# Second mixture of experts in hand order: raw weight pages loaded over a whole expert, split half an expert later

## The chip, the cores and the metric

The kernel runs on one core of one Trainium2 chip. The metric is the device time of one execution in microseconds; of several runs the median is given. A run's profile gives the span from the first to the last instruction and the granted clock of TensorE, as a share of its full 2.4 GHz.

## The reference

Windowed attention (window 64, 4 x 8 heads of 576 rows, head size 64) gives `x` of 2304 tokens by 512. A first, dense gated layer (`silu(xn @ w_gate) * (xn @ w_val) @ w_out` after an RMS norm) follows, and then the part that is changed, a second layer of eight experts of which each token takes two:

```python
logits = x @ w_gate
noise_scale = np.log1p(np.exp(x @ w_noise))
noisy_logits = logits + noise_scale * noise
top2 = np.argpartition(-noisy_logits, 2, axis=1)[:, :2]
...
for e in range(E):
    for k in range(2):
        mask = top2[:, k] == e
        ...
        h = np.maximum(x[mask] @ w1[e], 0.0)
        out[mask] += top2_w[mask, k, None] * (h @ w2[e])
```

Here `w1[e]` is 512 x 1024 and `w2[e]` 1024 x 512, in float32.

## The kernel before

Each float32 product is made of three matmuls in a faster format: an operand is split into a high part H (ScalarE copies it into that format) and a low part L (VectorE subtracts), and H*H, H*L and L*H are added up in PSUM. So every weight page that arrives raw (`st`, 128 x 1024) has to be split by ScalarE (`wH`, line 593) and then VectorE (`wL`, line 594) before TensorE can use it. The pages come from one pool of 24 (`page`); an expert has four raw pages of `w1` (i = 0 to 3) and four of `w2` (i = 4 to 7), which become 16 split pages. A page is free again when its last reader is done.

After the router, experts are taken by falling count, each with a fixed number of token slots: 640, 704, 640, 560, 560, 544, 544, 544. Position 0 is always expert 0. For position `e` there are these steps:

- `load_tb`: GpSimd fetches the table of token numbers and weights of the expert (`tb`); VectorE turns the numbers into integers (`tid`).
- `gather(e, t)`: GpSimd fetches 128 token rows (`xg`, L632); `xg_t(e, t)`: TensorE transposes them (`xgt`, L660), ScalarE writes their H part (`xph`, L663) and VectorE the L part (`xpl`, L664). For expert 0 these are `xah`/`xal` (first 384 slots) and `xbh`/`xbl` (the rest).
- `mm1(e, fc, blk)`: first product, L686, twelve matmuls into one PSUM bank `h` for 128 of the 1024 hidden columns and one half of the tokens; 16 such groups per expert. ScalarE (L693) and VectorE (L694) evict it as `hh`. Five banks are shared by these groups and by `xgt`.
- `mm2(e, t)`: second product of one tile of 128 tokens, L855, 24 matmuls of 512 columns into `y`; ScalarE scales it into `ys` (L862); GpSimd scatters it by a DMA that adds to `out` (L863). The scatters of different tiles add to the same tensor, so each waits for the one before.

An expert has five tiles (six at position 1), the last one with 32 to 64 tokens. The raw pages of experts 1 to 7 are loaded by GpSimd's indirect DMA (L584), those of expert 0 by SyncE.

Engines execute their own queues in order. What stands in the queues is set by a scheduler with a timeline model that reorders the program; the code below gives it only data dependencies and a program order to start from. In that order an expert's `mm2` tiles alternate with load and split of the next expert's `w1`, and `w2` follows behind the last tile:

```python
        for t in range(tiles(e + 1) if nx else len(left)):
            if left:
                mm2(e, left.pop(0))
            if nx:
                if t < 4:
                    load_split(e + 1, t)
                xg_t(e + 1, t)
```

Of the kernel before, what the change touches and what calls it, by code (L numbers as in the profile page):

```python
# [23 lines left out]
def tile_window_attention_swiglu_top2(  # L24
# [45 lines left out]
    def page(dt, name):  # L70
        return pages.tile([P, 1024], dt, name=name, tag="pg", bufs=NPG)
# [6 lines left out]

# [1 line left out]
    ident = consts.tile([P, P], F32, name="ident")  # L80
# [42 lines left out]

# [1 line left out]
    RG = 3 * WIN  # L125
# [16 lines left out]
    RT = (13, 14, 16, 17, 20)  # L142
    M2 = (2, 2)
    FL = (0, 0, 0, 1, 0, 0, 2)
# [128 lines left out]

# [1 line left out]
    xnH, xnL = {}, {}  # L275
# [52 lines left out]

# [1 line left out]
    gv, wo = {}, {}  # L330
# [101 lines left out]

# [1 line left out]
    XS, XTT, LZ = {}, {}, {}  # L434
# [136 lines left out]

# [1 line left out]
    W1, W2 = {}, {}  # L573
# [3 lines left out]

    def load_split(e, i):
        st = page(F32, f"st{e}_{i}")
        src, c = (w1r, i) if i < KD else (w2r, i - KD)  # L580
        if e == 0:
            nc.sync.dma_start(st, src[c * P:(c + 1) * P, :])
        else:
            nc.gpsimd.indirect_dma_start(out=st, out_offset=None, in_=src,  # L584
                                         in_offset=bass.IndirectOffsetOnAxis(ap=wi[:, e, c:c + 1], axis=0))
        h, l = page(F32R, f"wH{e}_{i}"), page(F32R, f"wL{e}_{i}")
        if i < KD:
            a, ho, lo = (x.rearrange(r, **{k: 2, "m": P}) for x, r, k in
                         ((st, "p (c m k) -> p c k m", "k"), (h, "p (c k m) -> p c k m", "k"),
                          (l, "p (c k m) -> p c k m", "k")))  # L590
        else:
            a, ho, lo = st, h, l
        nc.scalar.activation(ho, a, AF.Copy)  # L593
        nc.vector.tensor_tensor(lo, a, ho.bitcast(F32), op=ALU.subtract)  # L594
        if i < KD:
            W1[e, i] = (h, l)
        else:
            for k in range(2):
                W2[e, 2 * (i - KD) + k] = (h[:, 512 * k:512 * k + 512], l[:, 512 * k:512 * k + 512])

    XG, XH = {}, {}
# [15 lines left out]
    def load_tb(e):  # L617
# [3 lines left out]
        else:  # L621
            nc.gpsimd.indirect_dma_start(out=t.rearrange("p c w -> p (c w)"), out_offset=None,
                                         in_=table.rearrange("(p c) w -> p (c w)", c=NT1),
                                         in_offset=bass.IndirectOffsetOnAxis(ap=tbi[:, e:e + 1], axis=0))
        i = w2p.tile([P, 8], I32, name=f"tid{e}", tag="tid", bufs=2)
        nc.vector.tensor_copy(i[:, :tiles(e)], t[:, :tiles(e), 0])
        TB_[e], TID[e] = t, i

# [67 lines left out]

# [1 line left out]
    load_qk(0)  # L698
# [146 lines left out]
    def mm2(e, t):  # L845
# [5 lines left out]
        for fc in range(NF2):  # L851
            hh = HH[e, fc, part]
            h, l = W2[e, fc]
            for a, b in ((hh[:, 0, c], h), (hh[:, 0, c], l), (hh[:, 1, c], h)):
                nc.tensor.matmul(ps[:m], a, b, start=i == 0, stop=i == 3 * NF2 - 1)  # L855
                i += 1
        if e == 0 and t < TA:
            y, w, r = page(F32, f"ysa{t}")[:, :DM], ta[:, t, 1:2], tia[:, t:t + 1]
        else:
            y = w2p.tile([P, DM], F32, name=f"ys{e}_{t}", tag="ys", bufs=3)  # L860
            w, r = TB_[e][:, t, 1:2], TID[e][:, t:t + 1]
        nc.scalar.activation(y[:m], ps[:m], AF.Copy, scale=w[:m])  # L862
        nc.gpsimd.indirect_dma_start(  # L863
            out=out, out_offset=bass.IndirectOffsetOnAxis(ap=r[:m], axis=0),
# [6 lines left out]
    for fc in first:  # L871
        mm1(0, fc, 0)
    for t in range(M2[0]):
        mm2(0, t)
    main.close()

# [1 line left out]
    w2p = ctx.enter_context(tc.tile_pool(name="moe2", bufs=1, reuse_waits="tile"))  # L878
    V = nc.vector
    load_tb(0)  # L880

# [1 line left out]
    def row(name, n=E, dt=F32):  # L883
# [35 lines left out]

# [1 line left out]
    def count_beyond():  # L921
# [75 lines left out]


    for t in range(TA, tiles(0)):
        gather(0, t)  # L1000
    for t in range(M2[0], M2[1]):
        mm2(0, t)
    for t in range(TA, tiles(0)):
        xg_t(0, t)
    for t in range(M2[1], TA):
        mm2(0, t)
    for fc in range(NF2):
        mm1(0, fc, 1)
    for e in range(E):
        nx = e + 1 < E  # L1010
        if e > 0:
            for fc in range(NF2):
                for blk in range(2):
                    mm1(e, fc, blk)
        for kk in range(KD):
            W1.pop((e, kk))
        if nx:
            load_tb(e + 1)
            for t in range(tiles(e + 1)):
                gather(e + 1, t)  # L1020
        else:
            count_beyond()
        left = list(range(TA if e == 0 else 0, tiles(e)))
        for t in range(tiles(e + 1) if nx else len(left)):
            if left:
                mm2(e, left.pop(0))
            if nx:
                if t < 4:
                    load_split(e + 1, t)
                xg_t(e + 1, t)  # L1030
        for t in left:
            mm2(e, t)
        if nx:
            for i in range(4, 8):
                load_split(e + 1, i)

# [33 lines left out]
```

## Time and profile before

| | before |
|---|---|
| runs, us | 1153.52, 1159.80, 1159.81 |
| median, us | 1159.8 |
| span of the profiled execution, us | 1152.4 (no other time of that execution is recorded) |
| mean granted TensorE clock | 0.974 |
| TensorE busy | 1071.3 us, 93% of the span |
| VectorE, ScalarE, GpSimd busy | 53%, 48%, 38% |
| first product of expert 1 begins | 706.5 us into the span |

The page's slices show TensorE at nine tenths nearly throughout; what lies between two slices has to be looked for in the views of waits and in the timeline. In a timeline row the first number is the start, the second the length (of several merged instructions together), and the bracket tells how long the engine had been idle before it and what released it. "xN" is a number of merged instructions. Matmuls overlap, so the pace of TensorE is the distance from one start to the next, not the length.

### The profile page before, as it was taken

To read this page: it belongs to the slowest core of one execution; us is meant where nothing else is said; L and a number is where in the kernel's file an instruction comes from. 1 tells how busy PE (TensorE), PEld (TensorE's weight loads), DVE (VectorE), ACT (ScalarE), POOL (GpSimd) and SP (SyncE) were. 2 spreads that over 40 slices of the span, in tenths; PEclk is the share of its full clock that TensorE was granted. 3 is DMA by queue.
4 is the path that set the end of the run, shared out by engine and by line. 5 is a ranking of instruction groups with operands and counts; after the bars stand their busy time and mean duration, and the time that the engine had idled before them with its cause. 6 is when DMAs were issued, how large, how long until landed. Compare 5 with 4: busy or idle time off the path is not lost. (4 is left out here: it accounts for less than half of the span.)

```text
span 1152.4 us, 17705 instructions
## 1 busy us (share of the span) xinstructions
PE 1071.3 (93%) x6500; PEld 947.9 (82%) x6500; DVE 607.2 (53%) x1566; ACT 550.9 (48%) x1259; POOL 439.7 (38%) x456
## 2 busy tenths in 40 slices
PE   6788899999999999999999998998989898989994
PEld 5677688989989989998999887977878786969893
DVE  4899995765656566575776524523323242324210
ACT  7778765655656655665535224423324233323320
POOL 4366742342252253236223255233343524334211
PEclk9799999999999999999999998999999999989997
DMA  7956516201211120200203055453443443444302
GB/s 172 257 163 199 155 59 198 54 15 50 48 37 43 35 50 15 56 1 2 65 19 119 29 113 161 134 114 97 101 128 96 102 119 83 121 85 123 66 10 30
DMA packets 116376, 101.51 MB, mean 88 GB/s; under 512 B 82048, under 2 KB 94576, under 8 KB 116288
## 3 DMA queue, kind: packets, MB, share of 16 engines
q0 software_dynamic: 17872, 48.94, 17.8%
q1 hardware_dynamic: 98416, 51.42, 15.9%
q8 instruction: 52, 0.85, 0.3%
q14 instruction: 36, 0.29, 0.1%
HBM read 80.48 MB, written 19.85 MB: 87 GB/s over the span
## 5 line engine op out<-in xcount | busy, mean ns | idle before, releaser
L855 PE MATMUL y<-wH,hh 128*128 128x512 f32 (+3 forms) x656 | 215.4, 400 | 5.4 <-ACT hh L693 5.4
L398 PE MATMUL gv<-xnH,gvH 128*128 128x384 f32 x576 | 204.4, 356 | 4.2 <-ACT xnH L325 3.2
L398 PE MATMUL gv<-xnH,gvL 128*128 128x384 f32 x576 | 196.5, 343 | 4.2 <-DVE gvL L375 4.2
L398 PE MATMUL gv<-xnL,gvH 128*128 128x384 f32 x576 | 196.7, 342 | 0.0
L431 PE MATMUL x<-woHL,hh 128*128 128x512 f32 x648 | 174.9, 405 | 5.2 <-ACT hh L416 4.7
L686 PE MATMUL h<-xph,wH 128*128 128x272 f32 (+3 forms) x448 | 136.9, 308 | 25.2 <-ACT xph L663 19.9
L594 DVE TENSOR_TENSOR wL<-st,wH 128x1024 fp32r<-128x1024 f32 x64 | 78.3, 1224 | 147.9 <-ACT wH L593 141.2
L384 POOL TENSOR_TENSOR woHL<-wo,woHL 128x512 fp32r<-128x512 f32 x72 | 99.0, 1376 | 147.7 <-ACT woHL L383 147.5
L855 PEld LDWEIGHTS y<-wH,hh 128*128 128x128 f32 (+3 forms) x656 | 116.8, 179 | 40.0 <-ACT hh L693 5.8
L431 PEld LDWEIGHTS x<-woHL,hh 128*128 128x128 f32 x648 | 119.5, 190 | 28.6 <-ACT hh L416 5.8
L593 ACT ACTIVATE wH<-st 128x1024 fp32r<-128x1024 f32 x64 | 70.1, 1095 | 141.6 <-DMA st<-in_moe_w_dram,wi 124.0
L686 PE MATMUL h<-xpl,wH 128*128 128x272 f32 (+3 forms) x448 | 136.1, 304 | 0.1
L686 PE MATMUL h<-xph,wL 128*128 128x272 f32 (+3 forms) x448 | 135.8, 304 | 0.0
L863 POOL DMA_INDIRECT out_dram<-ys,tid x38 | 60.5, 1593 | 186.6 <-ACT ys L862 132.6
L855 PE MATMUL y<-wL,hh 128*128 128x512 f32 (+3 forms) x328 | 129.9, 397 | 0.0
L398 PEld LDWEIGHTS gv<-xnH,gvH 128*128 128x128 f32 x576 | 109.5, 190 | 7.8 <-ACT xnH L325 4.0
L693 ACT ACTIVATE hh<-h 128x160 fp32r<-128x160 f32 (+9 forms) x184 | 58.7, 342 | 118.1 <-PE h L686 85.1
L398 PEld LDWEIGHTS gv<-xnH,gvL 128*128 128x128 f32 x576 | 109.5, 190 | 6.1 <-DVE gvL L375 5.6
L398 PEld LDWEIGHTS gv<-xnL,gvH 128*128 128x128 f32 x576 | 109.8, 191 | 0.8
L694 DVE SCALAR_TENSOR_TENSOR hh<-h,hh 128x160 fp32r<-128x160 f32 (+9 forms) x184 | 64.7, 369 | 86.4 <-ACT hh L693 71.5
L686 PEld LDWEIGHTS h<-xph,wH 128*128 128x128 f32 x448 | 87.4, 196 | 26.9 <-ACT xph L663 20.8
L375 DVE TENSOR_TENSOR gvL<-gv,gvH 128x1024 fp32r<-128x1024 f32 (+1 forms) x73 | 91.8, 1259 | 13.1 <-ACT gvH L372 11.7
(203 smaller groups left out, 1882.6 us busy)
## 6 DMA issues: line engine op xcount, KB each, us to landing
vw<-in_v_dram SPq DMA_DIRECT2D x60, 128.0 KB, 2.8
raw<-in_moe_w_gate_dram SPq DMA_DIRECT2D x12, 512.0 KB, 7.5
raw<-in_moe_w_val_dram SPq DMA_DIRECT2D x12, 512.0 KB, 5.0
raw<-in_moe_w_out_dram SPq DMA_DIRECT2D x12, 512.0 KB, 4.1
out_dram<-zero SPq DMA_DIRECT2D x1, 4864.0 KB
qs<-in_q_dram SPq DMA_DIRECT2D x48, 96.0 KB, 2.6
ks<-in_k_dram SPq DMA_DIRECT2D x48, 96.0 KB, 2.7
x2d<-xs SPq DMA_DIRECT2D x18, 256.0 KB, 2.0
```

The source lines that it names most:

```text
L375: eng.tensor_tensor(l[:, f], gv[fc][:, f], h[:, f].bitcast(F32), op=ALU.subtract)
L384: nc.gpsimd.tensor_tensor(o[:, 512:], wo[fc], o[:, :512].bitcast(F32), op=ALU.subtract)
L398: nc.tensor.matmul(ps, a, b, start=n == 0, stop=n == 3 * KD - 1)
L431: nc.tensor.matmul(X2[j][t], a, b, start=fc == 0 and n == 0, stop=fc == NF - 1 and n == 2)
L593: nc.scalar.activation(ho, a, AF.Copy)
L594: nc.vector.tensor_tensor(lo, a, ho.bitcast(F32), op=ALU.subtract)
L686: nc.tensor.matmul(ps, w, x, start=i == 0, stop=i == 3 * KD - 1)
L693: nc.scalar.activation(hh[:, 0], v, AF.Relu)
L694: nc.vector.scalar_tensor_tensor(hh[:, 1], v, 0.0, hh[:, 0].bitcast(F32), op0=ALU.max, op1=ALU.subtract)
L855: nc.tensor.matmul(ps[:m], a, b, start=i == 0, stop=i == 3 * NF2 - 1)
L863: nc.gpsimd.indirect_dma_start(out=out, out_offset=bass.IndirectOffsetOnAxis(ap=r[:m], axis=0), in_=y[:m], in_offset=None, compute_op=ALU. ...
```

## The change

From expert 0's second token block on, the second layer is written under `manual_schedule`: every engine's queue then holds its instructions in the order of the code, and the code is written anew in that order. `load_split` is cut into `load_raw` (the DMA of a raw page) and `split_raw` (ScalarE and VectorE), and `mm2` into the product with its eviction and `scatter`. Two plans hang the side work on the products: `beside_first(e, n)` on the n groups of the first product (the splits of this expert's `w2` at shares 0, 0.2, 0.4 and 0.6; the next expert's table, its four `w1` pages at shares 0.125 to 0.875, its token ids and its first five gathers), and `beside_second(e, n)` on the n tiles of the second (the next expert's `w1` splits, its four `w2` loads and its `xg_t`). An expert's last scatter goes behind the next expert's first group. Tile 2 of expert 0 moves from ahead of that expert's second token block to behind it. In the changed kernel the line numbers from 585 on are 2 to 53 higher. The diff, cut to its core:

```diff
-    M2 = (2, 2)
+    M2 = 2
...
-    def load_split(e, i):
+    ST = {}
+
+    def load_raw(e, i):
         st = page(F32, f"st{e}_{i}")
...
+        ST[e, i] = st
+
+    def split_raw(e, i):
+        st = ST.pop((e, i))
         h, l = page(F32R, f"wH{e}_{i}"), page(F32R, f"wL{e}_{i}")
...
+    def load_split(e, i):
+        load_raw(e, i)
+        split_raw(e, i)
...
+        TB_[e] = t
+
+    def row_ids(e):
         i = w2p.tile([P, 8], I32, name=f"tid{e}", tag="tid", bufs=2)
-        nc.vector.tensor_copy(i[:, :tiles(e)], t[:, :tiles(e), 0])
-        TB_[e], TID[e] = t, i
+        nc.vector.tensor_copy(i[:, :tiles(e)], TB_[e][:, :tiles(e), 0])
+        TID[e] = i
...
+        SC[e, t] = (y, r, m)
+
+    SC = {}
+
+    def scatter(e, t):
+        y, r, m = SC.pop((e, t))
         nc.gpsimd.indirect_dma_start(
...
-    for t in range(M2[0]):
+    for t in range(M2):
         mm2(0, t)
+        scatter(0, t)
...
+    def beside_first(e, n):
+        plan = [[] for _ in range(n)]
+
+        def put(share, *f):
+            plan[min(int(share * n), n - 1)].append(f)
+
+        if e > 0:
+            for i in range(4):
+                put(0.0 + 0.2 * i, split_raw, e, 4 + i)
+        if e + 1 < E:
+            put(0.0, load_tb, e + 1)
+            for i in range(4):
+                put(0.125 + 0.25 * i, load_raw, e + 1, i)
+            put(0.4, row_ids, e + 1)
+            for t in range(min(tiles(e + 1), 5)):
+                put(0.45 + 0.12 * t, gather, e + 1, t)
+        return plan
+
+    def beside_second(e, n):
+        plan = [[] for _ in range(n)]
+        if e + 1 == E:
+            return plan
+        nt = tiles(e + 1)
+        for i in range(4):
+            k = min(i * (n - 1) // 3, n - 2)
+            plan[i * (n - 1) // 4].append((split_raw, e + 1, i))
+            plan[k].append((load_raw, e + 1, 4 + i))
+        for t in range(nt):
+            k = min(1 + t * (n - 1) // nt, n - 1)
+            plan[k].append((xg_t, e + 1, t))
+            if t + 5 < nt:
+                plan[k].append((gather, e + 1, t + 5))
+        return plan
+
+    def do(plan):
+        for f, *a in plan:
+            f(*a)
+
+    in_order = ExitStack()
+    in_order.enter_context(tc.manual_schedule())
     for t in range(TA, tiles(0)):
         gather(0, t)
-    for t in range(M2[0], M2[1]):
-        mm2(0, t)
     for t in range(TA, tiles(0)):
         xg_t(0, t)
-    for t in range(M2[1], TA):
-        mm2(0, t)
-    for fc in range(NF2):
-        mm1(0, fc, 1)
     for e in range(E):
-        nx = e + 1 < E
-        if e > 0:
-            for fc in range(NF2):
-                for blk in range(2):
-                    mm1(e, fc, blk)
+        groups = [(fc, blk) for fc in range(NF2) for blk in range(2) if e > 0 or blk == 1]
+        plan = beside_first(e, len(groups))
+        for g, (fc, blk) in enumerate(groups):
+            mm1(e, fc, blk)
+            if g == 0 and e > 0:
+                scatter(e - 1, tiles(e - 1) - 1)
+            do(plan[g])
         for kk in range(KD):
             W1.pop((e, kk))
-        if nx:
-            load_tb(e + 1)
-            for t in range(tiles(e + 1)):
-                gather(e + 1, t)
-        else:
+        if e + 1 == E:
             count_beyond()
-        left = list(range(TA if e == 0 else 0, tiles(e)))
-        for t in range(tiles(e + 1) if nx else len(left)):
-            if left:
-                mm2(e, left.pop(0))
-            if nx:
-                if t < 4:
-                    load_split(e + 1, t)
-                xg_t(e + 1, t)
-        for t in left:
+        left = list(range(M2 if e == 0 else 0, tiles(e)))
+        plan = beside_second(e, len(left))
+        for k, t in enumerate(left):
+            do(plan[k])
             mm2(e, t)
-        if nx:
-            for i in range(4, 8):
-                load_split(e + 1, i)
+            if e + 1 == E or k < len(left) - 1:
+                scatter(e, t)
+    in_order.close()
 
     trips = nc.values_load(tot[0:1, 0:1], min_val=0, max_val=N // P * 2)
     with tc.For_i(0, trips, 1):
```

What the built programs hold at three places (names are `name<expert>_<index>_<serial>`). First, **ScalarE at the step from expert position 3 to 4**, between the eviction of tile 3 and the first evictions of `hh4`; before:

```order
L862 ACTIVATE ys3_3_9307<-y3_3_9282,tb3_8616 128x512
L663 ACTIVATE xph4_9192<-xgt4_3_9318 128x4x128
L593 ACTIVATE wH5_0_9704<-st5_0_9702 128x1024
L862 ACTIVATE ys3_4_9350<-y3_4_9325,tb3_8616 48x512
L663 ACTIVATE xph4_9192<-xgt4_4_9355 128x4x48
L693 ACTIVATE hh4_0_0_9399<-h4_0_0_9386 128x280
L693 ACTIVATE hh4_1_0_9433<-h4_1_0_9420 128x280
L593 ACTIVATE wH5_1_9749<-st5_1_9747 128x1024
```

and now:

```order
L676 ACTIVATE xph4_9208<-xgt4_3_9298 128x4x128
L878 ACTIVATE ys3_3_9330<-y3_3_9305,tb3_8350 128x512
L676 ACTIVATE xph4_9208<-xgt4_4_9335 128x4x48
L878 ACTIVATE ys3_4_9367<-y3_4_9342,tb3_8350 48x512
L706 ACTIVATE hh4_0_0_9382<-h4_0_0_9369 128x280
L599 ACTIVATE wH4_4_9388<-st4_4_9165 128x1024
L706 ACTIVATE hh4_0_0_9382<-h4_0_1_9394 128x104
```

The split of the expert after (`wH5_0`) no longer stands ahead of `ys3_4` and `xph4_4`; the splits of `w2` (`wH4_4`) stand among the evictions of `hh4`.

Second, **GpSimd at the same step**, from the scatter of tile 3 on; before:

```order
L863 DMA out_0_dram<-ys3_3_9307,tid3_8618 2432x512
L584 DMA st5_0_9702<-in_moe2_w1_dram,wi_7438 128x1024
L584 DMA st5_1_9747<-in_moe2_w1_dram,wi_7438 128x1024
L863 DMA out_0_dram<-ys3_4_9350,tid3_8618 2432x512
L622 DMA tb5_9658<-table_67,tbi_7434 128x38
L632 DMA xg5_0_9662<-x2d_66,tid5_9660 128x512
L632 DMA xg5_1_9664<-x2d_66,tid5_9660 128x512
```

and now:

```order
L885 DMA out_0_dram<-ys3_3_9330,tid3_8466 2432x512
L885 DMA out_0_dram<-ys3_4_9367,tid3_8466 2432x512
L632 DMA tb5_9392<-table_67,tbi_7434 128x38
L586 DMA st5_0_9428<-in_moe2_w1_dram,wi_7438 128x1024
L586 DMA st5_1_9506<-in_moe2_w1_dram,wi_7438 128x1024
L645 DMA xg5_0_9528<-x2d_66,tid5_9508 128x512
L645 DMA xg5_1_9568<-x2d_66,tid5_9508 128x512
L586 DMA st5_2_9586<-in_moe2_w1_dram,wi_7438 128x1024
L645 DMA xg5_2_9606<-x2d_66,tid5_9508 128x512
```

The scatter of tile 4 is no longer behind two raw loads, the table comes ahead of them, and loads and gathers alternate. In the step from expert 0 to 1 the sixth gather stands behind a scatter and two loads now:

```order
L885 DMA out_0_dram<-ys0_2_7656,tia_100 2432x512
L586 DMA st1_6_7665<-in_moe2_w2_dram,wi_7438 128x1024
L586 DMA st1_7_7671<-in_moe2_w2_dram,wi_7438 128x1024
L645 DMA xg1_5_7682<-x2d_66,tid1_7539 64x512
L885 DMA out_0_dram<-ys0_3_7723,tid0_7408 2432x512
L885 DMA out_0_dram<-ys0_4_7774,tid0_7408 2432x512
```

Third, **TensorE at expert 0's second token block**, round the transposes of its tiles 3 and 4; before:

```order
L855 MATMUL y0_2_7467<-wH0_6_7180,hh0_4_0_7291 128x512
L855 MATMUL y0_2_7467<-wH0_6_7180,hh0_5_0_7307 128x512
L660 MATMUL xgt0_3_7451<-ident_68,xg0_3_7447 128x128 x4
L855 MATMUL y0_2_7467<-wL0_6_7181,hh0_5_0_7307 128x512
L660 MATMUL xgt0_4_7460<-ident_68,xg0_4_7449 128x128 x4
L855 MATMUL y0_2_7467<-wH0_6_7180,hh0_5_0_7307 128x512
L855 MATMUL y0_2_7467<-wH0_7_7186,hh0_6_0_7323 128x512
```

and now:

```order
L868 MATMUL y0_1_7372<-wL0_7_7187,hh0_7_0_7339 128x512
L868 MATMUL y0_1_7372<-wH0_7_7186,hh0_7_0_7339 128x512
L673 MATMUL xgt0_3_7453<-ident_68,xg0_3_7449 128x128 x4
L673 MATMUL xgt0_4_7462<-ident_68,xg0_4_7451 128x128 x4
L699 MATMUL h0_0_1_7469<-xbh0_7458,wH0_0_6465 128x256
L699 MATMUL h0_0_1_7469<-xbl0_7459,wH0_0_6465 128x256
```

The matmuls of tile 2 (`y0_2`) that stood between and behind the transposes are gone from there; they follow behind the second block's last group.

## Rows read from the trace of the kernel before

**Rows 1.** Waits of TensorE from 640 us on: who for whom, total, times, longest.
```profile
PE h L686 <- ACT xph L663: 19.9, 4, 5.4
PE y L855 <- ACT hh L693: 5.4, 1, 5.4
PE h L686 <- DVE hh L694: 5.3, 2, 3.7
```

**Rows 2.** Timeline of ScalarE: start, duration, engine, line, out<-in, idle before and releaser.
```profile
797.56 1.12 ACT L593 ACTIVATE wH<-st 128x1024 fp32r<-128x1024 f32 x1 [7.57 <-DMA st<-in_moe_w_dram,wi]
...
905.57 1.12 ACT L593 ACTIVATE wH<-st 128x1024 fp32r<-128x1024 f32 x1 [9.66 <-DMA st<-in_moe_w_dram,wi]
906.59 0.67 ACT L862 ACTIVATE ys<-y,tb 48x512 f32<-48x512 f32 x1
907.16 0.31 ACT L663 ACTIVATE xph<-xgt 128x192 fp32r<-128x192 f32 x1
```

**Rows 3.** Timeline of TensorE, 900 to 912 us.
```profile
900.10 0.40 PE L855 MATMUL y<-wL,hh 128*48 128x512 f32 x1
900.34 0.39 PE L855 MATMUL y<-wH,hh 128*48 128x512 f32 x1
...
907.52 0.68 PE L686 MATMUL h<-xph,wH 128*128 128x280 f32 x2 [4.68 <-ACT xph L663]
908.00 0.43 PE L686 MATMUL h<-xpl,wH 128*128 128x280 f32 x1
...
911.03 0.34 PE L686 MATMUL h<-xph,wL 128*128 128x280 f32 x1
911.21 0.29 PE L686 MATMUL h<-xph,wH 128*128 128x280 f32 x1
911.34 0.29 PE L686 MATMUL h<-xpl,wH 128*128 128x280 f32 x1
```

**Rows 4.** Timelines of GpSimd and VectorE, 836 to 901 us.
```profile
836.77 1.56 POOL L863 DMA_INDIRECT out_dram<-ys,tid  x1 [3.98 <-DMA out_dram<-ys,tid]
...
869.95 1.22 DVE L594 TENSOR_TENSOR wL<-st,wH 128x1024 fp32r<-128x1024 f32 x1
870.09 1.89 POOL L584 DMA_INDIRECT st<-in_moe_w_dram,wi  x1 [8.85 <-PE h L686]
...
898.18 1.57 POOL L863 DMA_INDIRECT out_dram<-ys,tid  x1 [4.04 <-issue]
900.05 1.01 POOL L584 DMA_INDIRECT st<-in_moe_w_dram,wi  x1 [0.30 <-issue]
```

**Rows 5.** Stretches: length, busy time of each engine, granted clock, DMA share, GB/s.
```profile
695.60:699.00 3.40, 3.38 (x10) 2.79 (x11) 2.83 (x4) 2.40 (x4) 1.03 (x1) 0.50 0.10 41
800.40:805.30 4.90, 4.88 (x23) 4.90 (x24) 2.27 (x7) 2.57 (x6) 0.00 (x0) 0.65 0.00 0
907.50:911.10 3.60, 3.58 (x16) 3.58 (x17) 1.07 (x3) 0.55 (x2) 2.71 (x2) 0.53 0.23 27
907.52:969.28 61.76, 56.80 (x332) 49.07 (x332) 20.56 (x39) 20.80 (x43) 23.47 (x19) 0.97 0.43 106
```

**Rows 6.** Timelines where expert 0's second block starts, 666 to 674 us.
```profile
666.06 0.96 POOL L632 DMA_INDIRECT xg<-x2d,tid  x1 [0.30 <-issue]
667.33 0.95 POOL L622 DMA_INDIRECT tb<-table,tbi  x1 [0.30 <-DVE cum L930]
670.85 0.17 DVE L626 CAST tid<-tb 128x6 int32<-128x6 f32 x1 [3.42 <-DMA tb<-table,tbi]
670.94 0.60 PE L660 MATMUL xgt<-ident,xg 128*128 128x128 f32 x4
671.29 0.48 PE L855 MATMUL y<-wL,hh 128*128 128x512 f32 x1
673.68 0.64 PE L686 MATMUL h<-xbh,wH 128*128 128x256 f32 x4
```

**Rows 7.** The weight loads of L584: count, min/median/max ns, first and last start.
```profile
L584 POOL DMA_INDIRECT st<-in_moe_w_dram,wi x56: 934/972/1891, 679.5 to 1069.5; - x56
```

More of the change, by code (lines that the diff above doesn't have):

```diff
@@ L856, in mm2 @@
                 i += 1
-        if e == 0 and t < TA:
-            y, w, r = page(F32, f"ysa{t}")[:, :DM], ta[:, t, 1:2], tia[:, t:t + 1]
+        if e == 0 and t < M2:
+            y = page(F32, f"ysa{t}")[:, :DM]
         else:
             y = w2p.tile([P, DM], F32, name=f"ys{e}_{t}", tag="ys", bufs=3)
+        if e == 0 and t < TA:
+            w, r = ta[:, t, 1:2], tia[:, t:t + 1]
+        else:
             w, r = TB_[e][:, t, 1:2], TID[e][:, t:t + 1]
         nc.scalar.activation(y[:m], ps[:m], AF.Copy, scale=w[:m])
+        SC[e, t] = (y, r, m)
+    SC = {}
+    def scatter(e, t):
+        y, r, m = SC.pop((e, t))
         nc.gpsimd.indirect_dma_start(
@@ L880, in tile_window_attention_swiglu_top2 @@
     load_tb(0)
+    row_ids(0)
     def row(name, n=E, dt=F32):
```

## Prediction, made before the changed kernel ran

> **What bounds the kernel now.** I began with the busy line of the page (the table above): TensorE is busy 93% of the span, so only its idle time and its slow time can be won. The view of who waited for whom, for TensorE from 640 us on, names them: four waits of about 5 us for ScalarE's `xph`, one of 5.4 for ScalarE's `hh`, and two of together 5.3 us for VectorE's `hh` [rows 1], in all 30.6 us. Ahead of 640 us the change moves nothing.
>
> ScalarE's timeline round 905 us shows what one such wait is [rows 2]. ScalarE stood 9.66 us idle for a raw weight page, split it (L593, 1.12 us), evicted `ys`, and only then wrote the 48 columns of `xph` for which TensorE had stood still 4.68 us [rows 3]. So the tokens were not late: they stood in ScalarE's queue behind a split whose page was late. GpSimd's rows say why the page was late [rows 4]: the load was issued at 900.05, after a scatter that began at 898.18 behind 4.04 us of idle. From 900.05 to 905.57 the page took 5.5 us to land. The order of instructions names that page: `wH5_0`, the first weight page of the expert after next, ahead of `xph4_4`. The same stands at the switches to the experts at positions 3 to 6. The waits for `hh` are of the same kind: at 797.56 ScalarE had stood 7.57 us for a raw page, with the evictions of the running product queued behind that split [rows 2].
>
> The clock is the second part. Behind the gap, matmuls of 280 columns start every 0.233 us (908.00 to 911.03, 13 steps), then every 0.13 (911.21 to 911.34) [rows 3]; the granted clock of that stretch is 0.53 [rows 5], that is nearly all the lower level of 1.2 GHz, after TensorE had stood idle.
>
> **The change, part by part: what it removes.** The waits: 30.6 us. No split stands ahead of a `xph` or a `ys` any more unless its page was issued about half an expert earlier (below), so all seven should go.
> The slow stretches: after 845.98, 907.52, 969.28 and 1030.70 there are 17, 16, 14 and 14 matmuls (one of the four stretches is shown [rows 5]) which lose 0.10 us each: 6.1. The stretch 695.60 to 699.00 ran at 0.50 of full speed, which loses half of 3.4: 1.7. From 800.40 to 805.30 the mean is 0.65; that is 3.4 us at half speed, a loss of 1.7 [rows 5]. Together 9.5. Taken off the span: 40.1.
>
> **What stays level.** TensorE's matmuls, ScalarE's and VectorE's splits, GpSimd's issues are as many as before. In one whole expert (907.52 to 969.28) VectorE was busy 20.6, ScalarE 20.8 and GpSimd 23.5 of 61.8 us [rows 5]; without gap and slow stretch TensorE needs 61.8 - 4.7 - 1.5 = 55.6. A second product of five tiles is 5 x 24 matmuls at 0.235 us (900.10 to 900.34 is one, [rows 3]), so 28 us; a first product is the other 27, or 1.6 to 1.7 per group of twelve.
>
> **Splits of w2, now beside the first product** at groups 0, 3, 6 and 9 of 16: 1.12 us on ScalarE and 1.22 on VectorE each [rows 2, 4], with the evictions of `hh` queued behind them, and TensorE behind those. Between two splits lie three groups, 5 us, of which a split takes a quarter; five banks hold five groups, about 8 us. I cost it at nothing; that cover is gone if a page is more than 8 us late. The last page is issued behind the third scatter of the second product, some 20 us into its 28, and is needed at group 9, another 8 + 15 us later: 23 us for a landing of 5.5.
> **Splits of w1, beside the second product**: loads go out at groups 2, 6, 10 and 14 of the first product, the splits come one ahead of each of the first four tiles. The nearest pair is the first: 14 groups, 23 us. The last: 2 groups and three tiles, 20 us. Nothing.
> **Scatters** move behind the raw loads on GpSimd, and the last of an expert behind the first group of the next. Each is 1.57 us of issue and waits for the scatter before it: 3.98 us at 836.77 [rows 4]. That is a chain of 5.6 us per tile, as long as TensorE's own tile (24 x 0.235 = 5.6); the loads of w2 go out inside these waits. With ten other issues (1.1 us and 0.3 between each) it is 5 x 5.6 + 14 = 42 us of 55.6: hidden, with 13 us to spare.
> **Token ids** (`row_ids`) are taken on VectorE a few groups after the table's load, so the 3.5 us from that issue to the copy (667.33 to 670.85 [rows 6]) no longer hold up VectorE. Nothing.
>
> **Start of the first expert: a new cost.** Tile 2 of expert 0 now comes after its second block, and its matmuls no longer cover the last two token tiles. From the first transpose (670.94) to the first product on them (673.68) 2.74 us passed, with TensorE full [rows 6]; of that only the two transposes, 0.35 each (670.94 to 671.29), remain as work, so 2.0 us of idle. Were the gathers later than that? The one issued at 666.06, with the 3.5 us of the table's load, lands at 669.6, no later than the transposes come. Six more of that tile's matmuls (6 x 0.235 = 1.4) filled the router's waits earlier and leave them open. I take 3.4; the bounds are 0 (the router's chain starts that much earlier) and 5.6 + 1.7 (the whole tile was cover, and the clock falls).
> **Step from expert 0 to 1: a new cost.** It has only three tiles left, so four splits, four loads and six token tiles crowd into them. The sixth gather is issued last, behind the scatter of tile 2 and two raw loads, and its transpose stands ahead of the last tile. From the end of tile 2 to that transpose TensorE has one tile and five transposes, 5.6 + 1.9 = 7.5 us; GpSimd has the eviction's 0.7, a scatter 1.6, two loads and the gather at 1.3 to 1.4 each, 6.3 in all, and then 3.5 us of landing: 9.8. So 2.3 us of waiting; bounds 0 and 5.5 + 1.7 (landing as slow as a raw page, and the slow stretch after).
> At this place the price of an issue is open. A raw load that began at 870.09, while VectorE was in a split from 869.95, took 1.89 us [rows 4], where the median is 0.97 [rows 7]. The Trainium skill, page "SBUF — State Buffer", section "SBUF: two separate sides", says that a VectorE instruction with two SBUF inputs and a GpSimd instruction that reads SBUF exclude each other for the whole instruction. By that rule, with which that row agrees, both splits at this place can each cost GpSimd up to their 1.22 us, and the sum below would be 2.4 us longer. I leave it out of the sum, since most issues of that kind in this trace show the plain duration (the median).
>
> **The sum.** Span 1152.4 - 40.1 + 3.4 + 2.3 = 1118.0. The record gives no time of its own for the profiled execution; its span lies 1.1 us below the lowest and 7.4 below the median of the three runs (1153.5 to 1159.8, median 1159.8). I add 7.4: **1125 us**, a gain of 3%. Less than 1% cannot be told from no change here, as the runs before differ by 0.5% themselves.
>
> **Rivals.**
> One: the wait moves into the first product. Raw pages of w2 land late, ScalarE stands at the split with `hh` behind it, and TensorE runs out of banks. For it: ScalarE waits for raw pages in nearly every split today. Against it: the distances of 20 us and more. If half of the present gap comes back at six switches, 6 x 3.2 = 19: 1145 us.
> Two: the change doesn't do what it says, because loads cannot run ahead: a page of the 24 is missing, and GpSimd waits for TensorE's last reading of an old page, as it does at 870.09 for 8.85 us [rows 4]. Then a late page holds up `xph` as now, and only the waits for `hh` with their slow stretches go (10.7 + 3.4) against 5.7 new: 1152 us. Against it, the count: at most 8 + 8 pages of weights in use and 4 raw are held at once in either half, 20 of 24.
> Three, slower than before: GpSimd's queue becomes the bound through the chain of scatters, as each raw load now lies ahead of a scatter and shares the DMA with it. An expert then takes 5c + 14, with c from scatter to scatter. At c = 5.6 it is 42 us; from c = 8.3 it passes TensorE's 55.6, and from c = 9.6 today's 61.8. At c = 10.5 it costs 66.5, 4.7 more than today in six experts: 1188 us. For it: the two waits of 4 us for a scatter before. Against it: they were with raw loads in flight too.
>
> **Chances.** Forecast 0.78, rival one 0.11, two 0.06, three 0.05. The forecast's own range runs from 1113 (no new cost, and the lesser offset of 1.1) to 1134 (both new costs at their upper bounds). To leave out no more than 2 in 10, the range reaches over about half of rival one, whose size is the least sure: 1113 to 1143. Faster by over 1% (below 1148): the forecast and most of rival one, 0.86. Within 1%: the rest of it and rival two, 0.09. Slower: rival three, 0.05.
>
> **What would show it.** Right: no wait of TensorE for `xph` at the later switches, a granted clock of 1.00 from expert 1's first product to the end, some 55.6 us from one expert to the next, ScalarE's waits for raw pages gone, and two short gaps left, ahead of the first product on expert 0's second block and ahead of its last tile. Wrong: TensorE waiting for `hh` with ScalarE at a split (rival one); GpSimd's loads waiting for TensorE in every expert, and `xph` late as now (two); scatter following scatter at more than 8 us and gathers issued only in the second product (three).

## The result and the profile after

The changed kernel takes 1124.8 us (median; 1124.4 to 1124.9), the kernel before, measured beside it, 1156.9 (1153.5 to 1159.8): a ratio of 0.9722, 95% interval 0.9696 to 0.9748. That is 2.8% faster, and 1125 was forecast. The profiled execution took 1124.9 with a span of 1123.1.

The view of who waited for whom, for TensorE from 640 us on, answers [rows 1]:

```profile
PE xgt L673 <- DMA xg<-x2d,tid: 5.3, 1, 5.3
PE rk L539 <- DVE pre L523: 1.0, 1, 1.0
PE h L699 <- ACT xbh L676: 0.8, 1, 0.8
PE lz L471 <- ACT ltT L468: 0.6, 1, 0.6
PE h L699 <- DVE xbl L677: 0.5, 1, 0.5
```

None of the seven waits of before is left. New are one for a gathered tile (5.3 us), two small ones where expert 0's second block starts (`xbh`, `xbl`) and one in the router at 653.4 us (`rk`), ahead of which 18 matmuls of the second product stand now and 27 stood before; the wait for `ltT` was there before.

The stretches (length, busy time of each engine, granted clock, DMA share, GB/s) answer [rows 5]:

```profile
711.00:1105.00 394.00, 394.00 (x2325) 343.43 (x2324) 139.25 (x267) 142.04 (x286) 142.82 (x120) 1.00 0.44 104
704.00:708.30 4.30, 4.27 (x13) 3.41 (x14) 0.42 (x1) 0.39 (x1) 0.00 (x0) 0.50 0.19 34
892.41:947.41 55.00, 55.00 (x334) 47.53 (x332) 20.54 (x38) 20.87 (x42) 22.28 (x19) 1.00 0.51 122
690.00:704.00 14.00, 8.76 (x49) 7.16 (x47) 5.67 (x8) 5.88 (x9) 7.98 (x7) 0.93 0.84 231
```

From 711 to 1105 us TensorE is busy in all 394.00 us at the granted clock 1.00 (2.4 GHz). The third line is one whole expert: 55.0 us, where before it was 61.8 with a gap and slow matmuls in it.

ScalarE's and TensorE's timelines at that expert's start (start, duration, engine, line, out<-in, idle before and releaser) answer [rows 2, 3]:

```profile
886.56 0.69 ACT L878 ACTIVATE ys<-y,tb 128x512 f32<-128x512 f32 x1 [3.91 <-issue]
887.14 0.32 ACT L676 ACTIVATE xph<-xgt 128x192 fp32r<-128x192 f32 x1
892.65 0.68 ACT L878 ACTIVATE ys<-y,tb 48x512 f32<-48x512 f32 x1 [5.19 <-issue]
...
894.46 1.05 ACT L599 ACTIVATE wH<-st 128x1024 fp32r<-128x1024 f32 x1
```

```profile
892.17 0.39 PE L868 MATMUL y<-wH,hh 128*48 128x512 f32 x1
892.41 0.29 PE L699 MATMUL h<-xph,wH 128*128 128x280 f32 x1
892.54 0.29 PE L699 MATMUL h<-xpl,wH 128*128 128x280 f32 x1
```

The last `xph` is written at 887.1, 5 us before TensorE needs it, and no split stands ahead of it. The first product follows the last tile after 0.24 us, and its matmuls start every 0.13 us at once, not every 0.23 as behind the gap before.

The one place that went worse is the step from expert 0 to 1. GpSimd, then VectorE, ScalarE and TensorE there, beside [rows 4]:

```profile
687.16 0.95 POOL L586 DMA_INDIRECT st<-in_moe_w_dram,wi  x1 [0.30 <-issue]
688.41 1.56 POOL L645 DMA_INDIRECT xg<-x2d,tid  x1 [0.30 <-issue]
690.27 0.95 POOL L586 DMA_INDIRECT st<-in_moe_w_dram,wi  x1 [0.31 <-issue]
691.52 0.95 POOL L586 DMA_INDIRECT st<-in_moe_w_dram,wi  x1 [0.30 <-issue]
694.64 1.62 POOL L885 DMA_INDIRECT out_dram<-ys,tia  x1 [2.17 <-ACT ys L878]
696.57 0.98 POOL L586 DMA_INDIRECT st<-in_moe_w_dram,wi  x1 [0.30 <-issue]
697.86 0.94 POOL L586 DMA_INDIRECT st<-in_moe_w_dram,wi  x1 [0.30 <-PE y L868]
699.10 0.93 POOL L645 DMA_INDIRECT xg<-x2d,tid  x1 [0.30 <-issue]
...
687.92 2.36 DVE L600 TENSOR_TENSOR wL<-st,wH 128x1024 fp32r<-128x1024 f32 x2 [0.60 <-ACT wH L599]
...
693.68 0.69 ACT L878 ACTIVATE ys<-y,ta 128x512 f32<-128x512 f32 x1 [4.75 <-PE xgt L673]
...
690.57 0.39 PE L868 MATMUL y<-wH,hh 128*128 128x512 f32 x1
...
704.03 0.66 PE L673 MATMUL xgt<-ident,xg 64*128 64x64 f32 x4 [5.27 <-DMA xg<-x2d,tid]
```

The last matmul of tile 2 is the one at 690.57. The sixth gather goes out at 699.10, behind that tile's scatter and two raw loads. TensorE stands 5.27 us until it has landed at 704.03, and then runs at half clock for 4.3 us (704.00 to 708.30 above).

### The profile page after: what moved, and what is told of

The parts are those of the page before. It is cut to its first block, busy times and chain, and to the rows that moved or that the text cites. A ratio compares the mean times of both kernels' runs of the same rounds, so it can differ in the third digit from the quotient of the medians.

```text
span 1123.1 us, 17720 instructions
## 1 busy us (share of the span) xinstructions
PE 1064.4 (95%) x6500; PEld 942.9 (84%) x6500; DVE 607.8 (54%) x1566; ACT 551.7 (49%) x1259; POOL 437.2 (39%) x456
## 3 DMA queue, kind: packets, MB, share of 16 engines
q1 hardware_dynamic: 98416, 51.42, 16.4%
## 5 line engine op out<-in xcount | busy, mean ns | idle before, releaser
L707 DVE SCALAR_TENSOR_TENSOR hh<-h,hh 128x160 fp32r<-128x160 f32 (+4 forms) x184 | 66.9, 371 | 140.7 <-ACT hh L706 125.6
L699 PE MATMUL h<-xph,wL 128*128 128x272 f32 (+3 forms) x448 | 132.9, 297 | 0.0
L699 PE MATMUL h<-xpl,wH 128*128 128x272 f32 (+3 forms) x448 | 132.9, 297 | 0.0
L699 PE MATMUL h<-xph,wH 128*128 128x272 f32 (+3 forms) x448 | 132.8, 296 | 0.0
L706 ACT ACTIVATE hh<-h 128x160 fp32r<-128x160 f32 (+4 forms) x184 | 61.4, 342 | 132.9 <-PE h L699 98.3
L878 ACT ACTIVATE ys<-y,tb 128x512 f32<-128x512 f32 (+3 forms) x38 | 26.1, 688 | 153.3 <-PE y L868 89.6
L375 DVE TENSOR_TENSOR gvL<-gv,gvH 128x1024 fp32r<-128x1024 f32 (+1 forms) x73 | 88.8, 1218 | 14.6 <-ACT gvH L372 12.3
L245 POOL TENSOR_TENSOR pm<-pm,st 128x384 f32<-128x384 f32 x48 | 41.1, 855 | 133.8 <-DVE st L244 96.2
```

Source lines behind the costliest of these rows:

```text
L245: nc.gpsimd.tensor_tensor(p, p, st[:, :, 3:4].to_broadcast([P, 3, P]), op=ALU.mult)
L375: eng.tensor_tensor(l[:, f], gv[fc][:, f], h[:, f].bitcast(F32), op=ALU.subtract)
L699: nc.tensor.matmul(ps, w, x, start=i == 0, stop=i == 3 * KD - 1)
L706: nc.scalar.activation(hh[:, 0], v, AF.Relu)
L707: nc.vector.scalar_tensor_tensor(hh[:, 1], v, 0.0, hh[:, 0].bitcast(F32), op0=ALU.max, op1=ALU.subtract)
```

## The experiments

Each kernel is the changed one with the edit shown, unless it says otherwise; ratios are to the kernel before, with their 95% interval.

| run | us | ratio |
|---|---|---|
| changed kernel | 1124.8 | 0.9722 [0.9696, 0.9748] |
| both raw loads at their splits | 1216.9 | 1.0496 [1.0461, 1.0531] |
| only w1 loaded at its split | 1170.3 | 1.0113 [1.0091, 1.0134] |
| only w2 loaded at its split | 1140.3 | 0.9839 [0.9810, 0.9868] |
| w1 loaded one tile ahead | 1125.2 | 0.9719 [0.9703, 0.9736] |
| scheduler's order | 1122.2 | 0.9686 [0.9669, 0.9702] |
| kernel before, loads written earlier | 1143.0 | 0.9881 [0.9862, 0.9901] |
| sixth gather first | 1115.5 | 0.9635 [0.9618, 0.9653] |
| the same under the scheduler | 1122.3 | 0.9696 [0.9678, 0.9715] |
| two w2 pages later | 1120.5 | 0.9678 [0.9661, 0.9694] |
| ten more gathers in the first product | 1198.3 | 1.0348 [1.0327, 1.0370] |
| ten memsets there | 1133.5 | 0.9798 [0.9765, 0.9831] |
| ten more gathers in the second product | 1122.5 | 0.9703 [0.9675, 0.9731] |

The theory was that the lead of the raw loads makes the gain. Its rivals were that the hand order does, or the moved tile. The moved tile was not run alone. But the first product of expert 1 begins at 712.24 us now and began at 706.51 before, so the whole gain falls behind that tile's last matmul.

**Both loads at their splits**, with everything else as changed:

```diff
-                put(0.0 + 0.2 * i, split_raw, e, 4 + i)
+                put(0.0 + 0.2 * i, load_split, e, 4 + i)
...
-            for i in range(4):
-                put(0.125 + 0.25 * i, load_raw, e + 1, i)
...
-            plan[i * (n - 1) // 4].append((split_raw, e + 1, i))
-            plan[k].append((load_raw, e + 1, 4 + i))
+            plan[i * (n - 1) // 4].append((load_split, e + 1, i))
```

> The hand order stays, but each raw page is loaded just ahead of its split (experts 1 to 7), not over the whole expert. Theory (a late raw page in ScalarE's queue is what cost the time): beside the second product each of four splits waits some 1.3 us of issue and 5.5 us of landing behind a scatter, 4 x 9 us in a second product of 28 us; TensorE then stands 5 to 9 us at each of seven switches with 1.5 us of slow clock after it, 1170 to 1200 us, slower than the kernel before too. The splits of w2 beside the first product stay hidden by the five banks. Rival (the order of the queues is what counts, not the lead of the loads): 1125 to 1135 us.

Measured: 1216.9 us, 92 more than the changed kernel and 58.5 more than the kernel before beside it. The hand order without the lead is worse than what it replaced; the size was underrated by 17 us. And the splits of `w2`, which the expectation took to stay hidden, did not: TensorE waited 34.3 us for `hh`.

**One half at a time:** the same edit for w1 alone, and for w2 alone.

> The changed kernel with one half undone: each raw page of w1 is loaded right ahead of its split beside the second product; the w2 pages keep their lead of half an expert. Loading both halves at the split cost 92 us against the changed kernel. Theory: a wait for a w1 page holds up ys and xph on ScalarE; a tile of 5.6 us stands against a page of 5.5 us to land, so each of the four waits is nearly covered by the tile before, and the loss is the smaller half: 6 steps of 3 to 6 us, 1143 to 1161. Rival: w1 is the larger half, since ScalarE's wait holds up the tokens of the next expert at once, 8 to 12 us a step: above 1172. If the two halves add up, this loss and that of the w2 half give 92.

> The changed kernel with the other half undone: each raw page of w2 is loaded right ahead of its split beside the first product; the w1 pages keep their lead. This is the prediction's rival one made real: ScalarE stands at the split with the evictions of hh queued behind it. The prediction held five banks, about 8 us of TensorE's work, against a landing of 5.5 us, and costed it at nothing. By that the time stays at 1125 to 1135. Theory after the run with both halves undone, where TensorE waited 34 us for hh: the banks don't cover it, as the split comes behind GpSimd's issue and each wait is followed by a slow stretch: 6 or 7 experts of 5 to 8 us, 1160 to 1180.

Measured: the w1 run takes 45.5 us more than the changed kernel, just under the rival's bound and well over my 18 to 36. The w2 run takes 15.5 more; its 1140.3 us lie between the prediction's 1125 to 1135 and my 1160 to 1180 and meet neither. That number also hides a part of the price. From the first product of expert 1 to the last matmul the w1 run and then the w2 run show (same columns as above):

```profile
719.26:1153.70 434.44, 410.78 (x2329) 354.07 (x2327) 139.58 (x267) 142.24 (x286) 139.27 (x120) 0.96 0.40 95
702.83:1123.60 420.77, 404.40 (x2329) 349.39 (x2327) 135.45 (x267) 136.19 (x286) 143.10 (x124) 0.98 0.42 103
```

The changed kernel takes 395.38 us for this, so in these experts w1 costs 39 us and w2 25. In the w2 run the wait of 5.3 us for the sixth gather is missing, since no early w2 load stands ahead of that gather, and with it the slow stretch. Both halves together cost 85 there, so they don't add up. In the w1 run ScalarE, GpSimd and TensorE at a later step:

```profile
840.74 1.14 ACT L599 ACTIVATE wH<-st 128x1024 fp32r<-128x1024 f32 x1 [7.83 <-DMA st<-in_moe_w_dram,wi]
...
842.26 0.68 ACT L878 ACTIVATE ys<-y,tb 128x512 f32<-128x512 f32 x1
...
850.76 1.12 ACT L599 ACTIVATE wH<-st 128x1024 fp32r<-128x1024 f32 x1 [7.82 <-DMA st<-in_moe_w_dram,wi]
...
843.22 1.61 POOL L885 DMA_INDIRECT out_dram<-ys,tid  x1 [5.87 <-ACT ys L878]
845.14 0.98 POOL L586 DMA_INDIRECT st<-in_moe_w_dram,wi  x1 [0.30 <-PE y L868]
...
851.93 0.48 PE L699 MATMUL h<-xph,wH 128*128 128x280 f32 x1 [4.19 <-ACT wH L599]
```

This is a loop through two queues: the page is issued behind a scatter (843.22), the scatter waits for `ys` (842.26), `ys` stands behind the split before (840.74), and that split waits for its own page. One round takes 10.0 us (840.74 to 850.76) where TensorE's tile takes 5.6. The lead cuts this loop. In the w2 run TensorE waits 16.4 us for `hh`, in twelve pieces of up to 2.9; one of them on ScalarE and TensorE:

```profile
891.17 0.41 ACT L706 ACTIVATE hh<-h 128x280 fp32r<-128x280 f32 x1 [0.82 <-PE h L699]
896.81 1.06 ACT L599 ACTIVATE wH<-st 128x1024 fp32r<-128x1024 f32 x1 [5.23 <-DMA st<-in_moe_w_dram,wi]
...
898.57 0.29 PE L699 MATMUL h<-xph,wL 128*128 128x280 f32 x1
900.17 0.37 PE L699 MATMUL h<-xph,wH 128*128 128x280 f32 x1 [1.31 <-DVE hh L707]
```

ScalarE stopped at 891.58 and TensorE ran on to 898.86: 7.3 us of cover, where the prediction took about 8 for five banks. The wait of 5.2 alone is shorter than that; the split and the `hh` that had queued up behind it came on top.

**How much lead:**

```diff
-            for i in range(4):
-                put(0.125 + 0.25 * i, load_raw, e + 1, i)
+            for i in range(4 if e == 0 else 1):
+                put(0.875 if e else 0.125 + 0.25 * i, load_raw, e + 1, i)
...
+            if e > 0 and i < 3:
+                plan[i].append((load_raw, e + 1, i + 1))
```

> Pages of w1 for experts 2 to 7 are loaded about one tile of the second product (5.6 us) ahead of their splits, not 20 us; w2 as in the changed kernel. Theory (what counts is landing plus queue, 5.5 to 7 us, against the lead): ScalarE waits 1 to 3 us for two or three pages per expert, and TensorE's cover of three y banks and the last tile hides it: 1124 to 1130 us. Rival (the lead of half an expert is needed): as in the run with the load at the split, 1150 us and more.

Measured: 1125.2, no difference, with ScalarE's longest wait for a page 2.2 us. A lead of one tile is enough for w1; half an expert isn't needed. For w2 a shorter lead was not tried in hand order.

**The order alone**, the scheduler ordering the new code:

```diff
-    in_order = ExitStack()
-    in_order.enter_context(tc.manual_schedule())
...
-    in_order.close()
```

> The changed code without the hand order: the scheduler orders the second layer, the early loads are in its program order. Its order again puts the next expert's first two splits ahead of the first evictions of the running one and a table's copy ahead of VectorE's evictions. Theory (lead of the loads): the page of the first such split is issued a whole second product earlier, the second's one some 6 us ahead, within the five banks' 8 us of cover, so most gaps stay away: 1122 to 1138 us. Rival (the hand order itself is needed): the waits for xph and hh come back, 1145 to 1157 us.

Measured: 1122.2. From the first product of expert 1 to the last matmul this run takes as long as the changed kernel (712.26 to 1107.22, there 712.24 to 1107.22), so the hand order brings nothing here. Then the other way round, **the kernel before with its loads written earlier**, in its own order:

```diff
         mm1(0, fc, 1)
+        if fc % 2:
+            load_raw(1, fc // 2)
...
+                if nx and fc % 2:
+                    load_raw(e + 1, fc // 2)
...
-                    load_split(e + 1, t)
+                    split_raw(e + 1, t)
+                    load_raw(e + 1, 4 + t)
...
-                load_split(e + 1, i)
+                split_raw(e + 1, i)
```

> The kernel before, in its own order under the scheduler, with one edit: the raw loads are written earlier in the code (w1 behind groups of the first product, w2 beside the tiles of the second), the splits stay where they were. The order of instructions shows that the scheduler still puts the first w1 page of the expert after next behind the scatter of tile 3 and its split ahead of the last eviction and the last xph, as in the kernel before. Theory (what counts is where the load stands in GpSimd's queue): the four waits for xph of 5 us and their slow stretches stay, those for hh go (10.7 + 3.4): 1140 to 1150. Rival (writing the loads earlier in the code is the whole gain): 1120 to 1130.

Measured: 1143.0, as expected, though not by the waits I named. GpSimd, ScalarE and TensorE in this run:

```profile
894.48 1.55 POOL L873 DMA_INDIRECT out_dram<-ys,tid  x1 [4.10 <-ACT ys L872]
896.34 1.01 POOL L586 DMA_INDIRECT st<-in_moe_w_dram,wi  x1 [0.31 <-PE y L865]
...
901.89 1.12 ACT L599 ACTIVATE wH<-st 128x1024 fp32r<-128x1024 f32 x1 [7.34 <-DMA st<-in_moe_w_dram,wi]
...
713.68 0.66 PE L696 MATMUL h<-xph,wH 128*128 128x352 f32 x1 [8.03 <-ACT xph L673]
...
903.84 0.52 PE L696 MATMUL h<-xph,wH 128*128 128x280 f32 x2 [2.41 <-ACT xph L673]
```

The load still stands behind the scatter and the split still ahead of `xph`, so the four waits are there, but at 2.4 to 3.1 us instead of 4.7 to 5.4; the step from expert 0 to 1 waits 12.0 (8.03 here, 4.00 ahead of a transpose) instead of 5.4. The two waits for VectorE's `hh` are gone, as expected. What counts is where a load and its split stand in the queues, not where the code has them.

**The sixth gather first**, and the first token tile with it, since the sixth needs that tile's buffer:

```diff
+        if nt > 5:
+            plan[0] += [(xg_t, e + 1, 0), (gather, e + 1, 5)]
-        for t in range(nt):
+        for t in range(1 if nt > 5 else 0, nt):
...
-            if t + 5 < nt:
-                plan[k].append((gather, e + 1, t + 5))
```

> At the step from expert 0 to 1 the first token tile is transposed ahead of expert 0's tile 2, and the sixth gather is issued right after it, ahead of that tile's scatter and of four raw loads. Theory (the gather came late because it was last in GpSimd's queue behind a scatter and two loads): the wait of 5.3 us and the 2.0 us of slow clock behind it go, 1117 to 1118 us. Rival (the six tiles and four pages are too much traffic for that place, and something else is late there): 1121 to 1125 us, with another wait near 700 us.

Measured: 1115.5, the fastest of all, 9.3 below the changed kernel and 1.5 below the range expected. The wait of 5.3 is gone, and with it the slow stretch (2.1): 7.4 that the edit made. The rest, some 2 us, is an earlier start and not the edit's: the wait for `ltT` ends at 642.27 here, at 644.39 in the changed kernel, at 642.53 before, and over all runs between 641.77 and 645.53, in code that no run touched. The same edit **under the scheduler**:

> The sixth gather written first in the step from expert 0 to 1, as in the run that gave 1115.5, but under the scheduler instead of the hand order. In the order of instructions the scheduler puts that gather back behind the scatter of tile 2 and two raw loads. Theory: no gain from it, 1120 to 1123 as under the scheduler without the edit, with TensorE waiting 3 to 5 us for that gather. Rival (the place in the code is enough): 1115 to 1117.

Measured: 1122.3, as without the edit (1122.2); TensorE waits 3.2 us for that gather and 2.9 for an `hh`. Here the hand order is needed.

**Why that gather was so late.** Tile 2's last matmul ends at 690.96, and its eviction starts only at 693.68. The edit moves the two raw loads at 690.27 and 691.52 behind the gather:

```diff
-            plan[k].append((load_raw, e + 1, 4 + i))
+            plan[k if e or i > 1 else n - 1].append((load_raw, e + 1, 4 + i))
```

> The changed kernel; in the step from expert 0 to 1 alone, the first two raw pages of w2 are loaded ahead of the last tile instead of ahead of tile 2. In the profile of the changed kernel the eviction of tile 2 starts 2.7 us after that tile's last matmul, while two such pages are in flight; with w2 loaded at the split it starts 0.4 us after. Theory: the pages in flight hold that eviction up, so without them the scatter and the sixth gather go out 2.7 us earlier, TensorE waits about 2.6 us for it instead of 5.3, and the time falls by 2.5 to 4: 1121 to 1122.5. Rival: the eviction waits for something else (the twelve transposes behind tile 2 on TensorE), the lag stays at 2.7 and the wait at 5.3: 1124 to 1125.5. The two pages now have one tile and a group, some 7 us, to land in 5.5; if that is too little a new wait for hh of 1 to 2 us shows at expert 1's first groups.

Measured: 1120.5. ScalarE's eviction and TensorE's wait:

```profile
689.71 0.69 ACT L878 ACTIVATE ys<-y,ta 128x512 f32<-128x512 f32 x1 [1.96 <-PE y L868]
...
700.20 0.43 PE L673 MATMUL xgt<-ident,xg 64*128 64x64 f32 x4 [2.77 <-DMA xg<-x2d,tid]
```

The eviction starts 0.1 us after the last matmul (689.62), and the wait is 2.8. Of the 4.3 us gained, 1.3 are an earlier start (the wait for `ltT` ends at 643.05). So the raw loads held ScalarE up, though ScalarE doesn't wait for them by name; by what means is not shown.

**GpSimd's queue**, the prediction's rival three. Behind each of five gathers of an expert stand two spare gathers of the small table:

```diff
+    def spare(e):
+        t = w2p.tile([P, NT1, 2], F32, name="sp", tag="sp", bufs=8)
+        nc.gpsimd.indirect_dma_start(out=t.rearrange("p c w -> p (c w)"), out_offset=None,
+                                     in_=table.rearrange("(p c) w -> p (c w)", c=NT1),
+                                     in_offset=bass.IndirectOffsetOnAxis(ap=tbi[:, e:e + 1], axis=0))
...
+                put(0.45 + 0.12 * t, spare, e + 1)
+                put(0.45 + 0.12 * t, spare, e + 1)
```

> The changed kernel with two spare gathers of the small table behind each of the first five gathers of an expert, into buffers that nobody reads: ten more issues of 0.95 us with 0.3 between, 12.5 us of GpSimd in every expert's first product. The prediction held GpSimd's queue to be hidden with 13 us to spare, of which this takes nearly all. By that the time stays at 1124 to 1128. Rival three (GpSimd's queue is close to the bound already): the scatter of each last tile and the w2 loads come late, and the time grows by 3 to 12 us an expert, 1145 to 1210.

Then memsets of 0.975 us in their place:

```diff
+    def spare():
+        nc.gpsimd.memset(w2p.tile([P, 1040], F32, name="sp", tag="sp", bufs=1), 0.0)
```

> The run with ten more issues (1198 us) again, at the same places, but with ten memsets of GpSimd of some 0.95 us each instead of ten spare gathers: the same time on GpSimd's queue, no DMA. In that run ScalarE's and TensorE's waits carried no name of GpSimd's, and began after 13 issues in a row. Theory (it was the row of indirect DMAs, not the time of GpSimd's queue): 1124 to 1128, the prediction's 13 us to spare hold. Rival three (GpSimd's queue is the bound): as with the spare gathers, 1185 to 1205.

And the spare gathers beside the tiles of the second product:

```diff
             plan[k].append((xg_t, e + 1, t))
+            if t < 5:
+                plan[k] += [(spare, e + 1)] * 2
```

> The ten spare gathers of the small table again, but two beside each tile of the second product, where each pair stands behind a scatter and a raw load, so that no more than six issues follow one another without GpSimd waiting for an eviction. Theory (a long row of issues without a pause holds up the other engines, not their number): 1124 to 1135. Rival (each extra indirect DMA costs about 1 us wherever it stands): 1185 to 1205.

Measured: 1198.3, 1133.5 and 1122.5. The first lies in rival three's range, the second in neither of its ranges, the third just below its own. The memset run lost its 8.7 us in the step from expert 0 to 1 alone, where the queue is short of time (a wait of 11.6 for the sixth gather); all later experts ran without a wait. So GpSimd's time is hidden, as predicted, outside of that step. The spare gathers in the second product cost nothing. In the first product they cost 73.5 us, 10.5 for each of the seven steps. At the step from expert 0 to 1 that is again a wait for the sixth gather (11.3). At the later ones the timelines of ScalarE and TensorE give only `remote` and `issue`, which name no instruction that was waited for:

```profile
906.56 0.26 ACT L712 ACTIVATE hh<-h 128x104 fp32r<-128x104 f32 x1 [9.50 <-remote]
...
894.12 0.29 PE L705 MATMUL h<-xph,wL 128*128 128x280 f32 x1
...
902.32 0.38 PE L679 MATMUL xgt<-ident,xg 128*128 128x128 f32 x2 [1.14 <-issue]
...
905.16 0.37 PE L679 MATMUL xgt<-ident,xg 128*128 128x128 f32 x1 [1.08 <-issue]
...
907.95 0.37 PE L679 MATMUL xgt<-ident,xg 128*128 128x128 f32 x1 [1.73 <-issue]
```

GpSimd issued 18 indirect DMAs without a pause from 883.49 to 905.58; TensorE had finished that `h` at 894.4, and ScalarE evicted it at 906.56, when the row was over. A long row by itself is not the cause, though, and my theory falls with that: in the second product 17 issues, four scatters among them, followed one another from 867.26 to 890.60 with 0.3 us between, not six as expected, and TensorE did not wait.

## Why the prediction came out right, step by step

**What bounded the kernel, and what went.** Right. The waits of 30.6 us are gone, and the slow stretches with them: the w1 run puts the loop back and the waits return. From the first product of expert 1 to the last matmul, before and now:

```profile
706.51:1137.15 430.64, 405.37 (x2329) 351.59 (x2328) 138.84 (x260) 141.13 (x288) 150.11 (x123) 0.98 0.42 99
712.24:1107.62 395.38, 395.37 (x2329) 343.45 (x2327) 139.25 (x267) 142.04 (x286) 142.82 (x120) 1.00 0.45 104
```

The time fell by 35.3 us; the terms for that part were 25.2 of waits and 7.8 of slow clock, 33.0. The idle time was 25.3, as summed. TensorE's busy time for the same matmuls fell by 10.0, so the slow clock had cost 2.2 more than the prediction counted.

**What was costed at nothing.** Splits of w2 and w1, scatters and token ids show no wait of TensorE in the changed kernel. Rival one (the wait moves into the first product) was made real in the w2 run: 25 us from expert 1 on, where it had 19. Rival two (no page free) did not happen: the 56 raw loads start 0.3 us behind the instruction before them. Their durations (least, median, most) answer [rows 7]:

```profile
L586 POOL DMA_INDIRECT st<-in_moe_w_dram,wi x56: 937/964/1277, 673.1 to 1046.6; - x56
```

Rival three did not happen either: scatter follows scatter after 5.7 to 7.0 us (868.90, 875.38, 882.36, 889.08, 894.77), under its 8.3. A longer chain by itself was not tried. Two slips of the working carry nothing: of w1's pairs of load and split the last, at its 20 us, is the nearest, not the first; and before, ScalarE waited for a raw page at 34 of the 56 splits, not at nearly every one.

**Start of expert 0's second block.** Forecast 3.4, measured 1.0 + 0.8 + 0.5 = 2.3.

**Step from expert 0 to 1: the term that was mis-sized.** Forecast 2.3, measured 5.3 and the slow stretch's 2.1, so 7.4, just past its upper bound of 7.2. The prediction had the place, the queue and the order right. It took the eviction of tile 2 as starting with that tile's end; it started 2.7 us later, which is nearly all of the 3.0 that the wait had more than forecast, and which moving two loads took away. The slow stretch stood in the bound alone.
On the price of an issue there: the gather at 688.41 took 1.56 us beside a split on VectorE, its neighbours 0.95, and the loads at 696.57 and 697.86 took the plain time. The Trainium skill, page "SBUF — State Buffer", section "SBUF: two separate sides", has such pairs exclude each other; the row at 688.41 agrees with it, at 0.6 us instead of the 2.4 that the whole splits would have cost. What an issue paid in these rows is about the rest of the split that was running when it began. At 688.41 the first of the two splits, by then 0.5 us old, had some 0.7 of its 1.2 left; the load at 696.57 began as such a split ended (695.42 to 696.65); and the load of [rows 4] at 870.09 had 1.1 us of a split left and took 0.9 over the median. The other way round these rows show no block: the split at 687.92 began beside the issue at 687.16, which ran to 688.11.

**The offset.** Forecast 7.4 from the span to the median; the profiled execution of the changed kernel took 1.8 more than its span. By that the profiled execution of before took some 1154.2, one of the short ones of its spread. The span fell by 29.3 instead of 34.4.

So the time was right by two errors that cancel: 5.6 too much in the offset; against it a span 5.1 too short, of which the step from expert 0 to 1 made 5.1, the start -1.1, an untouched stretch ahead of 644 us 1.9, and the rest -0.8. Either alone would have left the time inside the range. The mechanism was right; that the time came out within 0.2 us of the forecast is luck.

## What to carry to other kernels

Where a split or cast waits for a page on an engine that also evicts, issue the load ahead by at least one tile of the bounding engine (enough here for w1), and follow the circle: if the load stands behind a store that stands behind that same engine, each page costs the sum of the queue and not its landing time. Check it in the queues as built, since a scheduler can put an earlier written load back behind the store. Then look at the one irregular step, here the expert with a sixth tile; its gather was worth some 7 us of 1125.

## What the runs showed that was not expected

Extra indirect DMAs on GpSimd held up engines that wait for none of them. With 18 of them over the last part of the first product ScalarE evicted 12 us late and TensorE's transposes came 0.7 to 2.1 us apart; ten memsets of the same length in their place did neither, so it is the DMAs and not GpSimd's time. In the changed kernel two raw loads made one eviction 2.7 us late. But 17 issues in a row beside the second product did no harm. The amount of DMA traffic alone does not tell the two rows apart. While ScalarE stood still in the first product, and then beside the harmless row, the stretches show:

```profile
894.50:906.50 12.00, 7.75 (x31) 5.03 (x29) 0.45 (x1) 0.40 (x1) 9.26 (x10) 0.92 0.45 133
867.00:891.00 24.00, 24.00 (x112) 17.70 (x111) 6.43 (x8) 7.26 (x11) 18.86 (x17) 1.00 0.58 113
```

The DMA engines were busy 0.45 of the time where the others stood and 0.58 where they did not; round the late eviction of the changed kernel it was 0.84 (690 to 704 us). What carries it is open, and no run here shows it.
